# A Fourier mixing and GEGLU kernel: input tables without a setup pool, one batch's transposes in three PSUM buffers, output stores cut to multiples of sixteen rows

## The chip, the cores and the metric

One core of one Trainium2 chip. The metric is the device time of one execution in microseconds (us). The kernel before takes 1009.81 us (median of 4 runs, 1009.3 to 1010.2). Engines: PE is TensorE (PEld its weight loads), DVE VectorE, ACT ScalarE, POOL GpSimd, SP the engine that issues the output stores ("SPq" is its queue). A transfer by DMA is issued by an engine and lands when its data has arrived. An eviction copies a result of PE out of PSUM, the memory that PE writes, so that the buffer there is free again.

## The reference

```python
X = np.fft.fft(x, axis=1)          # x: (8, 3008, 256), float32
X = np.fft.fft(X, axis=2)
h = X.real.reshape(8 * 3008, 256)
g = h @ w_gate                     # (256, 1536)
gelu = 0.5 * g * (1.0 + erf(g / sqrt(2)))
out = (gelu * (h @ w_val)) @ w_out # (24064, 256), float32
```

## The kernel before

The transform over 3008 = 64 x 47 points is done with matmuls: stage 1 (64 points, table G2, result A_sb), transposes (Ap_sb), a 47-point stage (table T_PQ, result PQ_sb), and the transform over the 256 channels (tables C2 and S2, result Y_sb). A feed-forward part (ps_l, gelu_sb, h_sb, ps_o, out_sb) follows. There are eight batches. The feed-forward of batch b-1 is interleaved with the transform of batch b, so only the first transform and the last stores stand alone. These are the parts that matter (cuts marked with `# ...`):

```python
with tc.tile_pool(name="setup", bufs=1) as sp:     # released when the block ends
    # ... phases on 64 partitions, 47 x 33 columns, then the sines:
    nc.scalar.activation(G_all[:, :, 1, :], red_g, AF.Sin, scale=TWO_PI)
    # ...
    nc.scalar.activation(G_all[:, :, 0, :], red_g, AF.Sin, scale=-TWO_PI)
    nc.vector.memset(G2, 0.0)
    nc.vector.tensor_copy(...)                     # first half of G2 from G_all
    nc.sync.dma_start(                             # second half, other partitions
        out=_sub(G2, [[132, 23], [1, 66]], 66, part_start=64, part_num=64),
        in_=_sub(G_all, [[66, 23], [1, 66]], 24 * 66))
    # ... T_PQ, then C2 and S2, all with scratch of this pool

work_pool = ctx.enter_context(tc.tile_pool(name="work", bufs=1))
def x_tile():                                      # lies where the setup pool lay
    return work_pool.tile([128, 24, C], BF16, tag="x", bufs=2, name="x_sb")
def ps_tr():                                       # one buffer
    return psum_pool.tile([2 * N2, 1024], BF16, tag="tr", bufs=1, name="ps_tr")

# transposes, eight to a pack
pst = ps_tr()
for idx, (k1, cc) in enumerate(pk):
    nc.tensor.transpose(pst[:, idx * 128 : idx * 128 + 128], src, ident)
nc.scalar.activation(dst, pst[:, :n], AF.Copy)

# output of 128 tokens: cut where the row order of the output breaks
run_end = min(ue, ((ua // N2) + 1) * N2)           # N2 = 47
ln = run_end - ua                                  # mostly 47 rows or a part of 47
dst = ap_replace(out, ap=[[N1 * C, ln], [1, C]], offset=...)
nc.sync.dma_start(out=dst, in_=osb[p0 : p0 + ln, :])
```

## Time and profile before

| | before |
|---|---|
| time, median | 1009.81 us |
| first matmul | 27.19 us |
| stage 1 complete (A_sb) | 39.89 us |
| last transpose of batch 0 ends | 60.53 us |
| first matmul of the channel transform (C2) | 64.63 us |
| last matmul ends | 989.21 us |
| end of the span | 1007.72 us |

Times are from the start of the profiled span. Read the table as three pieces: 64.6 us until the channel transform begins, some 925 us that PE fills, and 18.5 us after the last matmul. The lines of the profile that carry this are shown in the prediction. One more is needed, on the output stores of the kernel before: the record of their issuing line gives the minimum, the median and the longest time, in ns, for which one issue held the queue.

```profile
L461 SPq DMA_DIRECT2D out_dram<-out_sb x696: 228/366/4578, 92.4 to 998.6; - x174
```

Half of the 696 issues are short, but the longest holds the queue for 4.6 us. Summed from the records, they hold it for 575.65 us.

### The profile page before, as it was taken

Reading aid. Unit: us, or ns where it says so; the run is one execution under the profiler, and the core shown is the slowest. Engines: PE = TensorE matmul, PEld = TensorE weight load, DVE = VectorE, ACT = ScalarE, POOL = GpSimd, SP = SyncE. Lnnn points to the kernel's source line nnn. Section 1 sums busy time; section 2 is a strip of 40 time slices with the busy share of each in tenths; the row PEclk is TensorE's granted clock in tenths of the full one; section 3 lists DMA queues with packets and bytes.
Section 4 is the critical chain, followed back from the end, with each engine's and each line's share of the span. In section 5 each row is a group of like instructions: output and inputs, shape, how many; then the busy total and the mean of one; then the engine's idle time right before and its main releaser. Section 6 shows DMA issues by size and latency. Waiting matters only on the chain.

```text
span 1007.7 us, 17222 instructions
## 1 busy us (share of the span) xinstructions
PE 943.1 (94%) x6304; PEld 611.6 (61%) x6304; DVE 590.2 (59%) x1122; ACT 502.5 (50%) x913; POOL 42.8 (4%) x81
## 2 busy tenths in 40 slices
PE   0579999999999999999999999999999999999991
PEld 0455766567656676657665676666665586555551
DVE  6457455773677547674567637765567735755550
ACT  2135554546454564555545464545545564555550
POOL 4300100010000100001000100000000000000000
PEclk9999999999999999999999999999999999999997
DMA  6900411013110411104110311101010101101110
GB/s 108 177 0 11 83 31 30 29 42 69 29 33 23 86 31 29 30 27 84 29 33 27 64 46 32 29 26 30 25 30 28 28 22 28 33 24 32 33 34 26
DMA packets 36093, 40.63 MB, mean 40 GB/s; under 512 B 5800, under 2 KB 31400, under 8 KB 36008
## 3 DMA queue, kind: packets, MB, share of 16 engines
q1 hardware_dynamic: 28792, 24.85, 8.8%
q0 software_dynamic: 7216, 14.68, 8.4%
q8 instruction: 49, 0.80, 0.3%
q14 instruction: 36, 0.29, 0.1%
HBM read 29.36 MB, written 24.64 MB: 54 GB/s over the span
## 4 chain that ended last, share of the span: by engine, by line
PE 89%; DVE 2%; DMA 2%; SPq 2%; ACT 1%; issue 1%; POOL 1%; ACTq 0%; POOLq 0%
PE ps_l L399 25%; PE ps_o L432 24%; PE ps_l L408 24%; PE ps_tr L288 8%; PE ps_dft L352 2%; PE ps_dft L344 2%; PE ps_dft L249 2%; SPq L461 2%; PE ps_dft L316 2%; DMA out_dram<-out_sb 2%; ACT Ap_sb L292 1%; DMA x_sb<-in_x_dram 1%; DVE PQ_sb L324 0%; DVE A_sb L265 0%; DVE A_sb L267 0%
## 5 line engine op out<-in xcount | busy, mean ns | idle before, releaser
L417 DVE TENSOR_TENSOR h_sb<-gelu_sb,ps_l 128x512 bf16<-128x512 bf16 (+1 forms) x576 | 386.2, 674 | 295.5 <-PE ps_l L408 144.7
L416 ACT ACTIVATE gelu_sb<-ps_l 128x512 bf16<-128x512 f32 (+1 forms) x576 | 334.1, 587 | 164.9 <-PE ps_l L399 159.9
L399 PE MATMUL ps_l<-Y_sb,Wg_sb 128*128 128x512 bf16 (+1 forms) x1152 | 342.7, 374 | 0.9
L408 PE MATMUL ps_l<-Y_sb,Wv_sb 128*128 128x512 bf16 (+1 forms) x1152 | 340.3, 374 | 0.3 <-ACT gelu_sb L416 0.3
L432 PE MATMUL ps_o<-Wo_sb,h_sb 128*128 128x256 bf16 (+1 forms) x2304 | 292.7, 272 | 2.3 <-ACT out_sb L440 1.4
L432 PEld LDWEIGHTS <-h_sb 128*128 128x128 bf16 (+1 forms) x2304 | 226.9, 99 | 68.1 <-issue 10.5
L408 PEld LDWEIGHTS <-Wv_sb 128*128 128x128 bf16 x1152 | 113.8, 100 | 114.3 <-issue 7.2
L440 ACT ACTIVATE out_sb<-ps_o 128x256 f32<-128x256 f32 x192 | 73.5, 383 | 191.1 <-PE ps_o L432 176.9
L399 PEld LDWEIGHTS <-Wg_sb 128*128 128x128 bf16 x1152 | 113.5, 102 | 79.2 <-issue 6.6
L288 PEld LDWEIGHTS <-A_sb 128*94 128x94 bf16 x528 | 99.8, 250 | 18.4 <-issue 6.9
L292 ACT ACTIVATE Ap_sb<-ps_tr 94x1024 bf16<-94x1024 bf16 (+1 forms) x72 | 68.2, 947 | 73.5 <-PE ps_tr L288 73.5
L288 PE MATMUL ps_tr<-ident,A_sb 128*94 128x128 bf16 x528 | 95.3, 311 | 7.8 <-ACT Ap_sb L292 6.8
L324 DVE CAST PQ_sb<-ps_dft 128x470 bf16<-128x470 f32 (+1 forms) x112 | 67.5, 613 | 31.9 <-PE ps_dft L316 31.9
L249 PE MATMUL ps_dft<-G,x_sb 128*128 128x132 bf16 x368 | 41.7, 232 | 32.5 <-DMA x_sb<-in_x_dram 31.4
L249 PEld LDWEIGHTS <-x_sb 128*128 128x128 bf16 x368 | 29.5, 102 | 53.1 <-issue 32.0
L362 DVE TENSOR_TENSOR Y_sb<-ps_dft,v_sb 128x470 bf16<-128x470 f32 x64 | 35.9, 560 | 42.7 <-ACT v_sb L360 42.6
L265 DVE CAST A_sb<-ps_dft 128x198 bf16<-128x198 f32 (+1 forms) x128 | 44.8, 350 | 18.5 <-PE ps_dft L249 17.7
L360 ACT ACTIVATE v_sb<-ps_dft 128x470 bf16<-128x470 f32 x64 | 31.6, 493 | 43.1 <-PE ps_dft L352 34.3
L316 PEld LDWEIGHTS <-Ap_sb 94*128 94x128 bf16 x528 | 36.5, 104 | 18.3 <-issue 0.2
L267 DVE CAST A_sb<-ps_dft 128x198 bf16<-128x198 f32 (+1 forms) x128 | 44.3, 346 | 0.0
L316 PE MATMUL ps_dft<-T_PQ,Ap_sb 94*128 94x94 bf16 x528 | 43.1, 214 | 0.1
L184 POOL DMA_DIRECT2D x_sb<-in_x_dram x32 | 17.8, 555 | 531.2 <-PE ps_dft L257 516.7
(60 smaller groups left out, 188.3 us busy)
## 6 DMA issues: line engine op xcount, KB each, us to landing
out_dram<-out_sb SPq DMA_DIRECT2D x328, 47.0 KB
x_sb<-in_x_dram POOLq DMA_DIRECT2D x56, 192.0 KB, 6.1
x_sb<-in_x_dram POOLq DMA_DIRECT2D x8, 160.0 KB, 7.7
Wg_sb<-in_moe_w_gate_dram POOLq DMA_DIRECT2D x1, 768.0 KB, 7.0
Wv_sb<-in_moe_w_val_dram POOLq DMA_DIRECT2D x1, 768.0 KB, 9.9
Wo_sb<-in_moe_w_out_dram POOLq DMA_DIRECT2D x1, 768.0 KB, 13.6
out_dram<-out_sb SPq DMA_DIRECT2D x8, 46.0 KB
out_dram<-out_sb SPq DMA_DIRECT2D x8, 45.0 KB
```

Of the source, the lines that this page charges most:

```text
L249: nc.tensor.matmul(ps[:, jj * 132 : (jj + 1) * 132], xt[:, j, cc * 128 : (cc + 1) * 128], G2[:, j, :], start=True, stop=True,)
L265: nc.vector.tensor_copy(dst, _sub(ps, [[132, np_], [1, 66]], 0))
L288: nc.tensor.transpose(pst[:, idx * 128 : idx * 128 + 128], src, ident)
L292: nc.scalar.activation(dst, pst[:, :n], AF.Copy)
L316: nc.tensor.matmul(ps[:, j * 94 : (j + 1) * 94], Ap[:, k1, cc * 128 : (cc + 1) * 128], T_PQ, start=True, stop=True,)
L324: nc.vector.tensor_copy(dst, ps[:, : g * 94])
L399: nc.tensor.matmul(psg[:, :ntok], Wg_sb[:, t, fc * 128 : (fc + 1) * 128], Yt[:, t, u0 : u0 + ntok], start=(t == 0), stop=(t == NCH - 1),)
L408: nc.tensor.matmul(psv[:, :ntok], Wv_sb[:, t, fc * 128 : (fc + 1) * 128], Yt[:, t, u0 : u0 + ntok], start=(t == 0), stop=(t == NCH - 1),)
L416: nc.scalar.activation(gl[:, :ntok], psg[:, :ntok], AF.Gelu)
L417: nc.vector.tensor_tensor(h[:, fc, :ntok], gl[:, :ntok], psv[:, :ntok], op=ALU.mult)
L432: nc.tensor.matmul(pso[:m, col0 : col0 + C], h[:, fc, sub * 128 : sub * 128 + m], Wo_sb[:, fc, :], start=(fc == 0), stop=(fc == NFC - 1),)
L440: nc.scalar.activation(osb[:m], pso[:m, col0 : col0 + C], AF.Copy)
```

## The change

The intent is to shorten both ends. At the start, the tables are made without a pool that the input's memory must wait for, and without a copy by DMA; the tables that only later stages need are made later; and the first batch's transposes get three PSUM buffers and two evicting engines. At the end, each store is cut into a multiple of 16 rows and a remainder. The diff, cut to its core:

```diff
-    G_all = const_pool.tile([N1, N2, 2, K1H], BF16)
-    G2 = const_pool.tile([128, 23, 2 * 66], BF16)
+    G2 = const_pool.tile([128, 24, 2 * 66], BF16)
-    with tc.tile_pool(name="setup", bufs=1) as sp:
-        ... (all tables, 47 x 33 columns on 64 partitions, DMA of half of G2)
+    scr_a = const_pool.tile([128, 24, K1H], FP32)     # and scr_b, scr_c, scr_d
 ...
-        for (j0, gj) in ((0, 6), (6, 6), (12, 6), (18, 6)):    # pieces of x
+        for j0 in range(0, 24, 3):
 ...
+    def ps_idle():
+        return psum_pool.tile([128, 1024], BF16, tag="l1", bufs=3, name="ps_idle")
+    ... (three iotas)
+    nc.gpsimd.memset(_sub(G2, [[132, 24], [1, 66]], 0, part_start=64, part_num=64), 0.0)
+    ... (three iotas)
+    load_x(0)
+    ... (loads of the weights, ident)
+    nc.vector.memset(_sub(G2, [[132, 24], [1, 66]], 66, part_start=0, part_num=64), 0.0)
+    ... (col_b, col_c)
+    nc.vector.tensor_scalar(row_t, row_j, col_c, 1.0 / T, op0=ALU.add, op1=ALU.mult)
+    for j in range(24):
+        nc.vector.tensor_scalar(scr_a[:, j, :], row_k, row_t[:, j : j + 1], None, op0=ALU.mult)
+    ... (reduction and four sines straight into G2)
 ...
-                pst = ps_tr()
+                pst = ps_idle() if b == 0 else ps_tr()
 ...
-                nc.scalar.activation(dst, pst[:, :n], AF.Copy)
+                if b == 0 and (pk[0][0] // 4) % 2 == 1:
+                    nc.vector.tensor_copy(dst, pst[: 2 * N2, :n])
+                else:
+                    nc.scalar.activation(dst, pst[: 2 * N2, :n], AF.Copy)
 ...
-                    nc.sync.dma_start(out=dst, in_=osb[p0 : p0 + ln, :])
+                    m16 = (ln // 16) * 16
+                    cuts = [(0, m16), (m16, ln - m16)] if hw else [(0, ln)]   # hw = True
+                    for (r0, rn) in cuts:
+                        if rn == 0:
+                            continue
+                        ... (dst of rn rows from row r0)
+                        eng.dma_start(out=dst, in_=osb[p0 + r0 : p0 + r0 + rn, :])   # nc.sync
 ...
+        if b == 0:                      # the later tables, among the work of batch 0
+            dw.insert(16, gen_tpq)
+            dw.insert(20, lambda: gen_c2s2(0))
+            dw.insert(24, lambda: gen_c2s2(1))
```

More of the change, by code (lines that the diff above doesn't have):

```diff
@@ L69 @@
     Wo_sb = const_pool.tile([128, NFC, C], BF16)
-    with tc.tile_pool(name="setup", bufs=1) as sp:
-        n1col = sp.tile([N1, 1], FP32)
-        nc.gpsimd.iota(n1col, pattern=[[0, 1]], base=0, channel_multiplier=1,
-                       allow_small_or_imprecise_dtypes=True)
-        n1scaled = sp.tile([N1, 1], FP32)
-        nc.vector.tensor_scalar(n1scaled, n1col, 1.0 / N1, None, op0=ALU.mult)
-        rowk1 = sp.tile([N1, N2, K1H], FP32)
-        nc.gpsimd.iota(rowk1, pattern=[[0, N2], [1, K1H]], base=0, channel_multiplier=0,
-                       allow_small_or_imprecise_dtypes=True)
-        rown2 = sp.tile([N1, N2, K1H], FP32)
-        nc.gpsimd.iota(rown2, pattern=[[1, N2], [0, K1H]], base=0, channel_multiplier=0,
-                       allow_small_or_imprecise_dtypes=True)
-        phase_g = sp.tile([N1, N2, K1H], FP32)
-        nc.vector.tensor_tensor(phase_g, rown2, rowk1, op=ALU.mult)
-        nc.vector.tensor_scalar(phase_g, phase_g, 1.0 / T, None, op0=ALU.mult)
-        nc.vector.scalar_tensor_tensor(phase_g, rowk1, n1scaled, phase_g,
-                                       op0=ALU.mult, op1=ALU.add)
-        tmp_g = sp.tile([N1, N2, K1H], FP32)
-        red_g = sp.tile([N1, N2, K1H], FP32)
-        nc.vector.tensor_scalar(tmp_g, phase_g, MAGIC, None, op0=ALU.add)
-        nc.vector.scalar_tensor_tensor(red_g, tmp_g, MAGIC, phase_g,
-                                       op0=ALU.subtract, op1=ALU.subtract)
-        nc.scalar.activation(G_all[:, :, 1, :], red_g, AF.Sin, scale=TWO_PI)
-        nc.vector.tensor_scalar(phase_g, phase_g, 0.25, None, op0=ALU.add)
-        nc.vector.tensor_scalar(tmp_g, phase_g, MAGIC, None, op0=ALU.add)
-        nc.vector.scalar_tensor_tensor(red_g, tmp_g, MAGIC, phase_g,
-                                       op0=ALU.subtract, op1=ALU.subtract)
-        nc.scalar.activation(G_all[:, :, 0, :], red_g, AF.Sin, scale=-TWO_PI)
-        nc.vector.memset(G2, 0.0)
-        nc.vector.tensor_copy(
-            _sub(G2, [[132, 23], [1, 66]], 0, part_start=0, part_num=64),
-            _sub(G_all, [[66, 23], [1, 66]], 0),
-        )
-        nc.sync.dma_start(
-            out=_sub(G2, [[132, 23], [1, 66]], 66, part_start=64, part_num=64),
-            in_=_sub(G_all, [[66, 23], [1, 66]], 24 * 66),
-        )
-        make_identity(nc, ident)
-        pcol94 = sp.tile([2 * N2, 1], FP32)
-        nc.gpsimd.iota(pcol94, pattern=[[0, 1]], base=0, channel_multiplier=1,
-                       allow_small_or_imprecise_dtypes=True)
-        rifl = sp.tile([2 * N2, 1], FP32)
-        nc.vector.tensor_scalar(rifl, pcol94, float(N2), None, op0=ALU.is_ge)
-        n2col = sp.tile([2 * N2, 1], FP32)
-        nc.vector.scalar_tensor_tensor(n2col, rifl, -float(N2), pcol94, op0=ALU.mult, op1=ALU.add)
-        nc.vector.tensor_scalar(n2col, n2col, 1.0 / N2, None, op0=ALU.mult)
-        ricol = sp.tile([2 * N2, 1], FP32)
-        nc.vector.tensor_scalar(ricol, rifl, -0.25, 0.25, op0=ALU.mult, op1=ALU.add)
-        rowk2 = sp.tile([2 * N2, 2, N2], FP32)
-        nc.gpsimd.iota(rowk2, pattern=[[0, 2], [1, N2]], base=0, channel_multiplier=0,
-                       allow_small_or_imprecise_dtypes=True)
-        qrow = sp.tile([2 * N2, 2, N2], FP32)
-        nc.gpsimd.iota(qrow, pattern=[[1, 2], [0, N2]], base=0, channel_multiplier=0,
-                       allow_small_or_imprecise_dtypes=True)
-        phase_t = sp.tile([2 * N2, 2, N2], FP32)
-        nc.vector.tensor_scalar(phase_t, rowk2, n2col, None, op0=ALU.mult)
-        nc.vector.scalar_tensor_tensor(phase_t, qrow, 0.25, phase_t, op0=ALU.mult, op1=ALU.add)
-        nc.vector.tensor_scalar(phase_t, phase_t, ricol, None, op0=ALU.add)
-        tmp_t = sp.tile([2 * N2, 2, N2], FP32)
-        red_t = sp.tile([2 * N2, 2, N2], FP32)
-        nc.vector.tensor_scalar(tmp_t, phase_t, MAGIC, None, op0=ALU.add)
-        nc.vector.scalar_tensor_tensor(red_t, tmp_t, MAGIC, phase_t,
-                                       op0=ALU.subtract, op1=ALU.subtract)
-        nc.scalar.activation(T_PQ[:, :], red_t, AF.Sin, scale=-TWO_PI)
-        pcol128 = sp.tile([128, 1], FP32)
-        nc.gpsimd.iota(pcol128, pattern=[[0, 1]], base=0, channel_multiplier=1,
-                       allow_small_or_imprecise_dtypes=True)
-        row256 = sp.tile([128, C], FP32)
-        nc.gpsimd.iota(row256, pattern=[[1, C]], base=0, channel_multiplier=0,
-                       allow_small_or_imprecise_dtypes=True)
-        pscal = sp.tile([128, NCH], FP32)
-        for cc in range(NCH):
-            nc.vector.tensor_scalar(pscal[:, cc : cc + 1], pcol128, float(128 * cc),
-                                    1.0 / C, op0=ALU.add, op1=ALU.mult)
-        phase_c = sp.tile([128, C], FP32)
-        tmp_c = sp.tile([128, C], FP32)
-        psin_c = sp.tile([128, C], FP32)
-        pcos_c = sp.tile([128, C], FP32)
-        xq_c = sp.tile([128, C], FP32)
-        for cc in range(NCH):
-            nc.vector.tensor_scalar(phase_c, row256, pscal[:, cc : cc + 1], None, op0=ALU.mult)
-            nc.vector.tensor_scalar(tmp_c, phase_c, MAGIC, None, op0=ALU.add)
-            nc.vector.scalar_tensor_tensor(psin_c, tmp_c, MAGIC, phase_c,
-                                           op0=ALU.subtract, op1=ALU.subtract)
-            nc.vector.tensor_scalar(xq_c, phase_c, 0.25, None, op0=ALU.add)
-            nc.vector.tensor_scalar(tmp_c, xq_c, MAGIC, None, op0=ALU.add)
-            nc.vector.scalar_tensor_tensor(pcos_c, tmp_c, MAGIC, xq_c,
-                                           op0=ALU.subtract, op1=ALU.subtract)
-            nc.scalar.activation(C2_sb[:, cc, :], pcos_c, AF.Sin, scale=-TWO_PI)
-            nc.scalar.activation(S2_sb[:, cc, :], psin_c, AF.Sin, scale=-TWO_PI)
@@ L168 @@
+    scr_a = const_pool.tile([128, 24, K1H], FP32)
+    scr_b = const_pool.tile([128, 24, K1H], FP32)
+    scr_c = const_pool.tile([128, 24, K1H], FP32)
+    scr_d = const_pool.tile([128, 24, K1H], FP32)
+    col_a = const_pool.tile([128, 1], FP32)
+    col_b = const_pool.tile([128, 1], FP32)
+    col_c = const_pool.tile([128, 1], FP32)
+    row_j = const_pool.tile([128, 24], FP32)
+    row_t = const_pool.tile([128, 24], FP32)
+    row_k = const_pool.tile([128, K1H], FP32)
     work_pool = ctx.enter_context(tc.tile_pool(name="work", bufs=1))
@@ L177, in load_x @@
         x_tiles.append(xt)
-        for (j0, gj) in ((0, 6), (6, 6), (12, 6), (18, 6)):
+        for j0 in range(0, 24, 3):
             src = ap_replace(
                 x,
-                ap=[[N2 * C, N1], [C, gj], [1, C]],
+                ap=[[N2 * C, N1], [C, 3], [1, C]],
                 offset=x.offset + (b * T + j0) * C,
             )
-            nc.gpsimd.dma_start(out=xt[0:N1, j0 : j0 + gj, :], in_=src)
-            gj2 = min(gj, 23 - j0)
+            nc.gpsimd.dma_start(out=xt[0:N1, j0 : j0 + 3, :], in_=src)
+            gj2 = min(3, 23 - j0)
             src = ap_replace(
@@ L230, in ps_tr @@
         return psum_pool.tile([2 * N2, 1024], BF16, tag="tr", bufs=1, name="ps_tr")
+    def ps_idle():
+        return psum_pool.tile([128, 1024], BF16, tag="l1", bufs=3, name="ps_idle")
+    nc.gpsimd.iota(col_a, pattern=[[0, 1]], base=0, channel_multiplier=1,
+                   allow_small_or_imprecise_dtypes=True)
+    nc.gpsimd.iota(row_j, pattern=[[1, 24]], base=0, channel_multiplier=0,
+                   allow_small_or_imprecise_dtypes=True)
+    nc.gpsimd.iota(row_k, pattern=[[1, K1H]], base=0, channel_multiplier=0,
+                   allow_small_or_imprecise_dtypes=True)
@@ new lines @@
+    rowk2_94 = const_pool.tile([2 * N2, 2, N2], FP32)
+    qrow_94 = const_pool.tile([2 * N2, 2, N2], FP32)
+    row256 = const_pool.tile([128, C], FP32)
+    nc.gpsimd.memset(_sub(G2, [[132, 24], [1, 66]], 0, part_start=64, part_num=64), 0.0)
+    nc.gpsimd.iota(rowk2_94, pattern=[[0, 2], [1, N2]], base=0, channel_multiplier=0,
+                   allow_small_or_imprecise_dtypes=True)
+    nc.gpsimd.iota(qrow_94, pattern=[[1, 2], [0, N2]], base=0, channel_multiplier=0,
+                   allow_small_or_imprecise_dtypes=True)
@@ new lines @@
+    nc.gpsimd.iota(row256, pattern=[[1, C]], base=0, channel_multiplier=0,
+                   allow_small_or_imprecise_dtypes=True)
+    load_x(0)
+    for w_hbm, w_sb in ((moe_w_gate, Wg_sb), (moe_w_val, Wv_sb)):
+        src = ap_replace(w_hbm, ap=[[F, 128], [128 * F, NCH], [1, F]], offset=w_hbm.offset)
+        nc.gpsimd.dma_start(out=w_sb, in_=src)
+    src = ap_replace(moe_w_out, ap=[[C, 128], [128 * C, NFC], [1, C]], offset=moe_w_out.offset)
+    nc.gpsimd.dma_start(out=Wo_sb, in_=src)
+    make_identity(nc, ident)
@@ new lines @@
+    nc.vector.memset(_sub(G2, [[132, 24], [1, 66]], 66, part_start=0, part_num=64), 0.0)
+    nc.vector.tensor_scalar(col_b, col_a, 64.0, -2984.0, op0=ALU.is_ge, op1=ALU.mult)
+    nc.vector.scalar_tensor_tensor(col_c, col_a, 47.0, col_b, op0=ALU.mult, op1=ALU.add)
+    nc.vector.tensor_scalar(row_t, row_j, col_c, 1.0 / T, op0=ALU.add, op1=ALU.mult)
+    for j in range(24):
+        nc.vector.tensor_scalar(scr_a[:, j, :], row_k, row_t[:, j : j + 1], None, op0=ALU.mult)
+    nc.vector.tensor_scalar(scr_b, scr_a, MAGIC, None, op0=ALU.add)
@@ new lines @@
+    nc.vector.scalar_tensor_tensor(scr_c, scr_b, MAGIC, scr_a, op0=ALU.subtract, op1=ALU.subtract)
+    for half in range(2):
+        p0 = half * 64
+        cb = half * 66
+        nc.scalar.activation(
+            _sub(G2, [[132, 24], [1, K1H]], cb + K1H, part_start=p0, part_num=64),
+            _sub(scr_c, [[K1H, 24], [1, K1H]], 0, part_start=p0, part_num=64),
+            AF.Sin, scale=TWO_PI,
+        )
+    nc.vector.tensor_scalar(scr_a, scr_a, 0.25, None, op0=ALU.add)
+    nc.vector.tensor_scalar(scr_b, scr_a, MAGIC, None, op0=ALU.add)
@@ new lines, with gen_tpq @@
+    nc.vector.scalar_tensor_tensor(scr_d, scr_b, MAGIC, scr_a, op0=ALU.subtract, op1=ALU.subtract)
+    for half in range(2):
+        p0 = half * 64
+        cb = half * 66
+        nc.scalar.activation(
+            _sub(G2, [[132, 24], [1, K1H]], cb, part_start=p0, part_num=64),
+            _sub(scr_d, [[K1H, 24], [1, K1H]], 0, part_start=p0, part_num=64),
+            AF.Sin, scale=-TWO_PI,
+        )
+    def gen_tpq():
+        pcol = col_a
+        rifl = _sub(col_b, [[1, 1]], 0, part_num=2 * N2)
+        n2col = _sub(col_c, [[1, 1]], 0, part_num=2 * N2)
+        p94 = _sub(pcol, [[1, 1]], 0, part_num=2 * N2)
+        nc.vector.tensor_scalar(rifl, p94, float(N2), None, op0=ALU.is_ge)
+        nc.vector.scalar_tensor_tensor(n2col, rifl, -float(N2), p94, op0=ALU.mult, op1=ALU.add)
+        nc.vector.tensor_scalar(n2col, n2col, 1.0 / N2, None, op0=ALU.mult)
+        ricol = _sub(col_b, [[1, 1]], 0, part_num=2 * N2)
+        nc.vector.tensor_scalar(ricol, rifl, -0.25, 0.25, op0=ALU.mult, op1=ALU.add)
+        ph = _sub(scr_a, [[1, 2 * N2]], 0, part_num=2 * N2)
+        tmp = _sub(scr_b, [[1, 2 * N2]], 0, part_num=2 * N2)
+        red = _sub(scr_c, [[1, 2 * N2]], 0, part_num=2 * N2)
+        nc.vector.tensor_scalar(ph, rowk2_94, n2col, None, op0=ALU.mult)
+        nc.vector.scalar_tensor_tensor(ph, qrow_94, 0.25, ph, op0=ALU.mult, op1=ALU.add)
+        nc.vector.tensor_scalar(ph, ph, ricol, None, op0=ALU.add)
+        nc.vector.tensor_scalar(tmp, ph, MAGIC, None, op0=ALU.add)
+        nc.vector.scalar_tensor_tensor(red, tmp, MAGIC, ph, op0=ALU.subtract, op1=ALU.subtract)
+        nc.scalar.activation(T_PQ[:, :], red, AF.Sin, scale=-TWO_PI)
@@ new lines, in gen_c2s2 @@
+    def gen_c2s2(cc):
+        pscal = col_b
+        nc.vector.tensor_scalar(pscal, col_a, float(128 * cc), 1.0 / C, op0=ALU.add, op1=ALU.mult)
+        ph = _sub(scr_a, [[1, C]], 0)
+        tmp = _sub(scr_b, [[1, C]], 0)
+        reds = _sub(scr_c, [[1, C]], 0)
+        redc = _sub(scr_d, [[1, C]], 0)
+        nc.vector.tensor_scalar(ph, row256, pscal, None, op0=ALU.mult)
+        nc.vector.tensor_scalar(tmp, ph, MAGIC, None, op0=ALU.add)
+        nc.vector.scalar_tensor_tensor(reds, tmp, MAGIC, ph, op0=ALU.subtract, op1=ALU.subtract)
+        nc.vector.tensor_scalar(ph, ph, 0.25, None, op0=ALU.add)
+        nc.vector.tensor_scalar(tmp, ph, MAGIC, None, op0=ALU.add)
+        nc.vector.scalar_tensor_tensor(redc, tmp, MAGIC, ph, op0=ALU.subtract, op1=ALU.subtract)
+        nc.scalar.activation(C2_sb[:, cc, :], redc, AF.Sin, scale=-TWO_PI)
+        nc.scalar.activation(S2_sb[:, cc, :], reds, AF.Sin, scale=-TWO_PI)
@@ L259, in run @@
                         _sub(xt, [[1, 128]], 23 * C + cc * 128, part_start=0, part_num=N1),
-                        G_all[:, 23, :, :],
+                        _sub(G2, [[1, 66]], 23 * 132, part_start=0, part_num=N1),
                         start=True,
@@ L284, in run @@
                 Ap = st["Ap"]
-                pst = ps_tr()
+                pst = ps_idle() if b == 0 else ps_tr()
                 for idx, (k1, cc) in enumerate(pk):
                     src = _sub(A, [[N2 * K1H, 2], [K1H, N2]], cc * AST + k1)
-                    nc.tensor.transpose(pst[:, idx * 128 : idx * 128 + 128], src, ident)
+                    nc.tensor.transpose(pst[: 2 * N2, idx * 128 : idx * 128 + 128], src, ident)
                 (k10, cc0) = pk[0]
@@ L455, in run @@
                         t0 = (N1 - k1) + N1 * j0
-                    dst = ap_replace(
-                        out,
-                        ap=[[N1 * C, ln], [1, C]],
-                        offset=out.offset + (b * T + t0) * C,
-                    )
-                    nc.sync.dma_start(out=dst, in_=osb[p0 : p0 + ln, :])
+                    hw = True
+                    m16 = (ln // 16) * 16
[3 more added lines that the diff above has]
+                            continue
+                        dst = ap_replace(
+                            out,
+                            ap=[[N1 * C, rn], [1, C]],
+                            offset=out.offset + (b * T + t0 + N1 * r0) * C,
+                        )
+                        eng = nc.sync if hw else nc.gpsimd
+                        eng.dma_start(out=dst, in_=osb[p0 + r0 : p0 + r0 + rn, :])
                     ua = run_end
@@ L475, in ffn_work @@
         return units
-    load_x(0)
-    for w_hbm, w_sb in ((moe_w_gate, Wg_sb), (moe_w_val, Wv_sb)):
-        src = ap_replace(w_hbm, ap=[[F, 128], [128 * F, NCH], [1, F]], offset=w_hbm.offset)
-        nc.gpsimd.dma_start(out=w_sb, in_=src)
-    src = ap_replace(moe_w_out, ap=[[C, 128], [128 * C, NFC], [1, C]], offset=moe_w_out.offset)
-    nc.gpsimd.dma_start(out=Wo_sb, in_=src)
     for b in range(B):
```

## The prediction

> **What bounds the kernel now.** I read the page's 40 slices first, to see where TensorE (PE) is not full, then a table of stretches cut at the places where the chain of work changes hands, then the waits, then the chain itself at both ends. PE is full from the third slice to the last but one, so only the two ends can give anything.
>
> ```profile
> span 1007.7 us, 17222 instructions
> PE   0579999999999999999999999999999999999991
> DVE  6457455773677547674567637765567735755550
> ```
>
> Table of stretches (length, then busy time and count of PE, weight load, DVE, ACT, POOL, then clock, DMA share, GB/s):
>
> ```profile
> 0.00:27.00 27.00, 0.00 (x0) 0.00 (x0) 17.30 (x34) 6.06 (x8) 14.07 (x26) 1.00 0.71 114
> 27.00:40.00 13.00, 7.42 (x50) 4.49 (x50) 9.04 (x34) 0.00 (x0) 4.72 (x10) 1.00 1.05 194
> 40.00:60.60 20.60, 13.85 (x97) 13.69 (x98) 3.24 (x5) 8.18 (x9) 3.32 (x7) 1.00 0.44 78
> 60.60:64.60 4.00, 3.75 (x38) 2.92 (x36) 3.87 (x8) 0.35 (x1) 0.00 (x0) 1.00 0.00 0
> 92.00:985.00 893.00, 890.87 (x5974) 576.31 (x5972) 534.99 (x994) 473.35 (x870) 20.74 (x40) 1.00 0.15 37
> 989.30:1007.80 18.50, 0.00 (x0) 0.00 (x0) 0.00 (x0) 0.38 (x1) 0.00 (x0) 0.60 0.07 25
> ```
>
> The middle, 92 to 985 us, is 890.87 of 893 us PE: nothing there can be hidden better, and the change leaves its matmuls alone. The start has 27 us with no matmul, then a stage at DVE's and the input's pace, then 20.6 us in which PE is a third idle. The end has 18.5 us with no PE work at all. The waits say why:
>
> ```profile
> POOL x_sb L184 <- ACT C_sb L165: 12.3, 1, 12.3
> PE ps_dft L249 <- DMA x_sb<-in_x_dram: 31.4, 4, 27.2
> PE ps_tr L288 <- ACT Ap_sb L292: 6.8, 8, 1.2
> ```
>
> The first line is the surprise: the first loads of x wait for the last sine (L165), though they don't use it. The x tile lies in the memory of the setup pool, so it may be written only when the last setup tile is read. Loads are issued from 22.59 us and the first matmul runs at 27.19. In the chain, transposes and their eviction alternate, because there is one buffer, ps_tr:
>
> ```profile
> 42.53 1.41 PE ps_tr L288 x8
> 43.97 1.03 ACT Ap_sb L292
> 45.04 1.42 PE ps_tr L288 x8
> 46.48 1.03 ACT Ap_sb L292
> ```
>
> So a pack takes 2.51 us of which PE works on transposes for 1.42. At the end of the chain:
>
> ```profile
> 957.91 1.89 SPq L461
> 959.84 1.94 SPq L461
> 966.12 8.74 DMA out_dram<-out_sb
> 983.47 7.26 DMA out_dram<-out_sb
> ```
>
> The output queue, not PE, is last. Issues that would take about 0.25 us hold it for 1.9, and a store lands 7 to 9 us after it is issued.
>
> [...] after 999 us its packet records show one 1 KB packet starting every 0.0425 us until 1006.0, a single engine draining; 47 such are 2.0 us, the 1.94 us that the queue stalls. [...] POOL took 0.74 to 1.04 us to issue each weight load while DVE was busy, 0.52 to 0.55 us for each load of x with DVE idle or reading PSUM; the shapes differ too. [...] the same two matmuls of 470 columns take 0.94 us at 64.6 and 0.56 us from 68.6 us.
>
> **The change, part by part.**
>
> *Tables and loads.* The tables for the first stage are made for both halves of the partitions at once (24x33 instead of 47x33 columns, no copy, no DMA of G), the others are made later, and all scratch is in the constant pool, so x waits for nothing. DVE, from 1.13 us, scaling its rows of 1551 and 256 columns (0.88 and 0.20 us between starts for a tensor_scalar, 1.68 and 0.34 for a scalar_tensor_tensor): zeroing half of G2 0.7 (1.32 us for 1518 words before, 792 now); small ones to 2.3; 24 operations of 33 columns at some 0.105 are 2.5, to 4.8; 0.5 and 0.2 of small ones, 5.5; 0.9, 6.4; then 0.5, 0.5, 0.9, to 8.3. ACT's four sines of 792 columns are 0.86 each (1.51 for 1551, 0.40 for 256): the last two end at 10.0. So the table is ready at 10 us, not at 20.5. DVE's other table work in its new order (T_PQ, a part of C2/S2, with a wait for ACT's read of scr_c) ends at 10.6.
>
> POOL: small iotas, zeroing the other half of G2 (an estimate of 1.4 us from 0.19 us for ident's 128 columns), three iotas, first x issue at 3.5 us; 16 issues at 0.52 us if undisturbed. Data moved from 1.4 us after the first issue, at 0.2 MB/us (190 to 218 KB in each full microsecond of the trace), so 1.54 MB need 7.5 us: last piece at about 14.5, or 16.5 if nine of the issues take 0.75.
>
> Stage 1 then goes at DVE's evictions: 34 of them, 4.4 us for the second 17 before (35.5 to 39.9), so 8.8, from 10.6 to 19.4. With the last x piece a little late I take 20.5, against 39.9: **19.4 us gained**.
>
> *Transposes.* ps_idle has three buffers, and DVE evicts four of nine packs (94x1024; an estimate of 1.2 us from 0.64 us for 470 and 0.36 for 198 columns). Neither ACT (1.02, and some sines of 0.4) nor DVE (1.2 and 0.9 of table work per two packs) needs the 2.84 us that PE needs for two packs. So PE sets it: 66 x 0.178 = 11.7, and in the new order of instructions only 7 of the 66 T_PQ matmuls lie between, 0.8 us: 12.5 instead of 20.6. But that order has one PQ eviction before the last transposes instead of six, so the tail of that stage grows: last transpose at 33.0, DVE free at 33.9, eight PQ evictions to the first C2 matmul, 4.2: it starts at 38.1, before at 64.63. **26.5 us gained in all at the start**, 7.1 of it here.
>
> *Stores.* Each run of rows is cut to a multiple of 16 and a remainder under 16[...]: 696 issues become 1256, but the rows on the busiest engine go from 18376 to 1704 (my count over all runs), or from 780 to 72 us at 0.0425. 1256 issues at 0.3 us are 377 us of the queue, less than the 576 us that they took before with the stalls, so no new bound. Per 128 rows there are 6 or 7 issues, 2.0 us or slightly over, for one every 1.95 us in bursts of four. At the end: PE's last matmul to the last eviction 0.4 (it waited 1.6 more for a store), backlog and four issues 1.6, landing 2.4 (0.8 from issue to first packet, 1.4 from the last packet to the end): 4.4 instead of 18.5 us. **14.1 us gained.**
>
> Sum: 26.5 + 14.1 = 40.6; 1009.8 - 40.6 = 969.2, called 969.5.
>
> **The rivals.** [...] the last piece lands at 19 and stage 1 ends at 24. For it: DVE is full just then[...]. Against it: the weights, issued while DVE was 99% busy, streamed at the full rate. It costs 3 to 4 us: 973. It also delays ident, which stands behind 19 loads on POOL. *PE warms early:* denser transposes [...] take about 0.135 us (four in 0.54 at 131.2 us): 3 us less, 966. Against it: [...]the trace shows 60 to 64 us[...] leaving it cold. *The store queue becomes the bound:* a store of 32 rows waits on one of eight semaphores; at a landing of 3 us that is 0.38 us each and a backlog of some 3 us at the end: 972. Should cutting not spread the stores, the end gains nothing: 983. *The gain at the start is given back later*, in the ramp at 77 to 92 us: weights now come after x, but the last land near 27 us and are first used near 43, so I give it little.
>
> **Range and chances.** The independent uncertainties are 3 to 4 us at the start on the slow side, 3 on the fast, and 2 to 3 at the end: 961 to 978. 2% is 20 us; either the start alone (26) gives that or the start's slow case with a small part of the end. Faster 0.97, same 0.03.
>
> **What would show it.** First matmul near 10 us, with the wait being for G2 or x and no ACT C_sb wait on POOL; A complete near 20; transposes with no wait on Ap evictions; first C2 matmul near 38; PE full after that; no store issue of 1.9 us; the end within 5 us of the last matmul. [...] I'm wrong if the first C2 matmul comes after 45, if PE's share in the middle falls under 99%, or if the last stores still take over 8 us.

## The result

| | before | after |
|---|---|---|
| time, median | 1009.76 us (13 runs, 1009.25 to 1010.2) | 972.71 us (8 runs, 972.4 to 973.55) |
| first matmul | 27.19 | 12.46 |
| stage 1 complete | 39.89 | 21.99 |
| last transpose of batch 0 ends | 60.53 | 33.12 |
| first C2 matmul | 64.63 | 39.47 |
| last matmul ends | 989.21 | 964.01 |
| end of the span | 1007.72 | 970.31 |
| from last matmul to the end | 18.5 | 6.3 |

The ratio is 0.9635, with a 95% interval of 0.9625 to 0.9644. Here and below a ratio is the mean time of one kernel's fast runs over that of the other's fast runs of the same rounds, so it is not quite the ratio of the medians quoted.

The span became 37.4 us shorter. The start gives 64.63 - 39.47 = 25.2 us of it and the end 18.5 - 6.3 = 12.2 us. The middle is unchanged: 924.6 us from the first C2 matmul to the last matmul before (989.21 - 64.63), 924.5 after (964.01 - 39.47). From the page of the kernel after, the span and PE's busy tenths in 40 slices:

```profile
span 970.3 us, 18209 instructions
PE   4999999999999999999999999999999999999996
```

The kernel before showed "057" at the left and "91" at the right. Now the first slice holds PE work, the second is full, and the last is more than half full. The table of stretches of the kernel after, cut at the same hand-overs, says what each is limited by (length, then busy time and count of PE, weight load, DVE, ACT, POOL, then clock, DMA share, GB/s):

```profile
0.00:12.40 12.40, 0.00 (x0) 0.00 (x0) 10.63 (x44) 4.98 (x6) 11.40 (x28) 1.00 0.62 90
12.40:22.00 9.60, 8.01 (x51) 4.61 (x51) 9.52 (x39) 0.53 (x2) 5.66 (x11) 1.00 1.06 186
22.00:33.10 11.10, 11.06 (x73) 11.06 (x74) 5.69 (x14) 4.99 (x7) 4.51 (x10) 1.00 1.19 182
33.10:39.50 6.40, 6.06 (x61) 4.75 (x59) 6.40 (x13) 0.38 (x1) 6.14 (x12) 1.00 1.07 166
92.00:960.00 868.00, 866.00 (x5798) 559.14 (x5797) 521.61 (x964) 460.52 (x847) 33.16 (x64) 1.00 0.16 36
964.00:970.40 6.40, 0.01 (x1) 0.00 (x0) 0.00 (x0) 0.38 (x1) 0.00 (x0) 0.76 0.15 36
```

The clock of 1.00 in the first four lines is no measurement: the trace's record of the granted clock begins only at 42.3 us, with full clock (in the kernel before at 68.2 us, so that the same holds for the early stretches in the prediction). Stage 1 (second line) is DVE's: 9.52 of 9.60 us busy. In the transposes (third line) PE is now full, 11.06 of 11.10, where it was a third idle. The fourth line is DVE's again, all 6.40 us, though PE looks busy there too. The middle is as full as before (866.00 of 868). The chain that ended last, at the start (start and length in us):

```profile
2.02 0.69 DVE row_t L175
2.82 3.60 DVE scr_a L177 x24
...
22.04 6.29 PE ps_idle L293 x37
...
32.83 0.69 DVE Ap_sb L298
33.52 5.91 DVE PQ_sb L332 x11
39.47 0.94 PE ps_dft L352 x2
...
43.25 0.57 PE ps_dft L352 x2
```

From 22.04 us the transposes no longer alternate with evictions; 37 follow each other. Two C2 matmuls still take 0.94 us at 39.47 and 0.57 only from 43.25. The end of the same chain shows the output queue:

```profile
958.63 0.32 SPq L476
...
962.58 1.46 DMA out_dram<-out_sb
```

No issue of 1.9 us is left there (the longest of the whole kernel is still 1.91 us), and a landing that the chain waits for takes 1.46 us, not 7 to 9. Two waits of the kernel after (in all, times, longest) are the ones to set against the waits of before:

```profile
ACT out_sb L448 <- DMA out_dram<-out_sb: 51.7, 46, 1.7
PE ps_dft L254 <- DVE scr_a L227: 12.5, 1, 12.5
```

POOL's wait for a sine is gone, and so is the chain's alternation with ps_tr. The second line is the wait for table G2. It names L227, an operation for a later table that merely ended at that moment; the last sine into G2 had ended at 12.21 us. The first line is new in size: the eviction of the output waits 51.7 us for its buffer to be stored, against 14.0 us in 13 waits before. It costs nothing, because ACT has room: PE waits 1.4 us in all for these evictions in both kernels, and the middle is as long as it was. Over all 1256 stores, from the record of the issuing line:

```profile
L476 SPq DMA_DIRECT2D out_dram<-out_sb x1256: 236/382/1912, 67.0 to 967.9; - x180
```

Almost twice as many issues hold the queue for 478.0 us in sum, less than the 575.65 us of before, and 22 instead of 242 take over 1 us.

### The profile page after: what moved, and what is told of

The parts are those of the page before. It is cut to its first block, busy times and chain, and to the rows that moved or that the text cites.

```text
span 970.3 us, 18209 instructions
## 1 busy us (share of the span) xinstructions
PE 943.2 (97%) x6304; PEld 610.9 (63%) x6304; DVE 588.9 (61%) x1148; ACT 498.6 (51%) x911; POOL 72.2 (7%) x144
## 4 chain that ended last, share of the span: by engine, by line
PE 94%; DVE 3%; SPq 1%; ACT 1%; DMA 1%; issue 0%; ACTq 0%; DVEq 0%
PE ps_l L407 27%; PE ps_o L440 25%; PE ps_l L416 25%; PE ps_tr L293 7%; PE ps_dft L360 2%; PE ps_dft L352 2%; PE ps_dft L254 2%; PE ps_dft L324 2%; PE ps_idle L293 1%; SPq L476 1%; DVE PQ_sb L332 1%; DMA out_dram<-out_sb 1%; DVE A_sb L272 0%; DVE A_sb L270 0%; DVE scr_a L177 0%
## 5 line engine op out<-in xcount | busy, mean ns | idle before, releaser
L293 PE MATMUL ps_tr<-ident,A_sb 128*94 128x128 bf16 x462 | 83.3, 304 | 0.0
L300 ACT ACTIVATE Ap_sb<-ps_tr 94x1024 bf16<-94x1024 bf16 (+1 forms) x63 | 59.7, 947 | 43.2 <-PE ps_tr L293 43.2
L97 POOL DMA_DIRECT2D x_sb<-in_x_dram x64 | 36.0, 562 | 473.9 <-PE ps_dft L262 468.1
L254 PE MATMUL ps_dft<-G,x_sb 128*128 128x132 bf16 x368 | 42.1, 232 | 14.2 <-DVE scr_a L227 12.5
```

The source lines that it names most:

```text
L254: nc.tensor.matmul(ps[:, jj * 132 : (jj + 1) * 132], xt[:, j, cc * 128 : (cc + 1) * 128], G2[:, j, :], start=True, stop=True,)
L293: nc.tensor.transpose(pst[: 2 * N2, idx * 128 : idx * 128 + 128], src, ident)
L300: nc.scalar.activation(dst, pst[: 2 * N2, :n], AF.Copy)
```

## The experiments

Twelve kernels ran. "After" or "before" says which kernel the edit starts from. Each time is a median of 4 runs, with 20 for the kernel that frees x alone; each ratio is to the kernel before. All results were correct.

**Is the end due to the cut of the stores, and do the two ends add?** From after, with the cut undone:

```diff
-                    m16 = (ln // 16) * 16
+                    m16 = ln
```

> The changed kernel with each run of rows stored whole again (the cut undone, nothing else). Theory (one DMA engine serves a store of 47 rows, and its backlog is the end): the gain at the end is given back and nothing else is, 972.7 + 12.2 = 985 us; queue issues of 1.9 us come back and the span ends about 18 us after the last matmul; the first C2 matmul stays at 39.5 us. Rival (the end is a fixed landing time, the gain came from elsewhere): within 2 us of 972.7.

Measured: 984.49 us (983.85 to 985.88), ratio 0.9753 [0.9737, 0.9769]. The start is unchanged (first C2 matmul at 39.46 us), and the end comes 18.1 us after the last matmul. The chain of this kernel at the end again has the lines of before:

```profile
953.55 1.93 SPq L476
...
957.79 7.38 DMA out_dram<-out_sb
```

The other direction, before with nothing but the cut:

```diff
-                    nc.sync.dma_start(out=dst, in_=osb[p0 : p0 + ln, :])
+                    m16 = (ln // 16) * 16
+                    for (r0, rn) in [(0, m16), (m16, ln - m16)]:
+                        ... (one store of rn rows from row r0)
```

> The kernel before with the stores cut alone. Theory (start and end are separate and add): 1009.8 - 12.2 = 997.6 us, the start as before (first matmul 27.2, first C2 matmul 64.6), the end 6.3 us after the last matmul. Rival (cutting also frees the middle or, the other way, its 1256 issues delay it): more than 1 us away from 997.6.

Measured: 997.95 us (997.72 to 998.33), ratio 0.9882 [0.9868, 0.9897]. The end comes 6.7 us after the last matmul and the start is that of before (C2 at 64.94 us). So the cut is worth 11.8 us with either start, and the two ends add.

**Is it the divisor, or only that stores are smaller and more?** In the traces of before and after, what follows a store depends on its row count. The landing record of each store has one update more than the largest divisor up to 16 of its row count, but never more than 16: 2 updates for 47, 41 or 23 rows, 3 for 46, 12 for 44, 16 for 15, 16, 32 or 45. So it is in all 696 stores before and all 1256 after. Whole runs also leave singly: the last 165 rows of before, parts of several stores, start one every 0.0425 us from 999.0 to 1006.0, with never more than two packets of 0.046 us open at once. In after up to 14 are open at once from 963.0 us on. A kernel with still more and still smaller stores whose divisor is low tells the divisor from size. From after, pieces of 23 rows, a prime:

```diff
-                    cuts = [(0, m16), (m16, ln - m16)] if hw else [(0, ln)]
+                    cuts = [(r0, min(23, ln - r0)) for r0 in range(0, ln, 23)]
```

> The changed kernel with each run cut into pieces of 23 rows and a remainder (47 = 23 + 23 + 1): more and shorter stores than the change makes, but 23 is prime. Theory [...]: the busiest engine gets as many rows as with whole runs or more (20992 by my count, against 18376 whole and 1704 cut), so the gain at the end is lost: 984 us or more. Rival (shorter stores, or more of them, are the gain): 972 to 974 us.

Measured: 1025.25 us (1023.22 to 1026.14), ratio 1.0153: slower than the kernel before, although the start is that of after. The stores of this kernel, as one issue's minimum, median and longest; then SP's wait for landings; then the middle stretch:

```profile
L476 SPq DMA_DIRECT2D out_dram<-out_sb x1536: 227/236/3412, 67.5 to 1016.5; - x192
```
```profile
SPq L476 <- DMA out_dram<-out_sb: 405.5, 746, 1.9
```
```profile
92.00:985.00 893.00, 860.98 (x5664) 556.25 (x5749) 517.35 (x956) 454.84 (x838) 34.17 (x66) 0.99 0.13 34
```

The median issue got shorter (236 ns), so the size isn't the matter. But SP waited 405.5 us for stores to land, and now the queue even holds up PE: 860.98 us busy of 893 where before had 890.87. Of the 52.5 us over after, 38.5 lie between the first C2 matmul and the last matmul, and 13.4 behind it. The prediction's count of rows on the busiest DMA engine divides each store's rows by that divisor and adds this up over all stores: 18376 for whole runs of rows, 20992 for pieces of 23, and 1704 for the cut of the change. It is an estimate: the records name no engine, and that all stores load the same one is taken from the 165 rows that left singly.

The number of packets on the output queue shows the divisor too. These are the lines of the pages (packets, MB, share of 16 engines) for whole runs, the change, the halves of the next experiment and the pieces of 23:

```profile
q1 hardware_dynamic: 27304, 24.65, 8.9%
q1 hardware_dynamic: 40960, 24.71, 10.2%
q1 hardware_dynamic: 33952, 24.68, 9.4%
q1 hardware_dynamic: 28048, 24.66, 7.3%
```

In each, 24064 packets are the output's rows of 1 KB. The rest, 3240, 16896, 9888 and 3984, have 4 bytes, and they are exactly the sum, over all stores, of the largest divisor up to 16 of the row count. This fits one short packet for each engine that serves a store, but the records name no engine.

That 14% more rows than with whole runs cost 40 us more is argued, not shown. At the 0.0425 us a row that the prediction read, 20992 rows are 892 us of the 949 between the first issue and the end of the last (an estimate), so that engine has hardly a pause left; 18376 rows are 781. Part of the loss is PE's clock: its record falls to half five times before the last matmul, for 27.2 us in all.

A middle case, from after, with two halves (47 = 23 + 24; 1384 stores, 10704 rows on the busiest engine by the same count):

```diff
-                    m16 = (ln // 16) * 16
+                    m16 = ln // 2
```

> The changed kernel with each run cut in two halves (47 = 23 + 24) instead of 32 + 15: about as many and as short stores. Theory [...] the stalls of the queue on pieces of 23 rows are about 1 us, and part of the backlog is left at the end: 974 to 981 us. Rival (shorter stores are the gain): equal to 972.7 within 1.

Measured: 973.98 us (973.79 to 974.12), ratio 0.9646 [0.9629, 0.9662]. That is 1.3 us over after, on the border of what the two theories expected. The end comes 7.5 us after the last matmul, against 6.3. By itself this run is inconclusive. It shows that 58% of the count of whole runs (10704 of 18376) is borne almost without loss, so the time isn't proportional to the count. Over the four ways to cut, the count (1704, 10704, 18376, 20992) and the time (972.7, 974.0, 984.5, 1025.3 us) rise together, while the number of stores (1256, 1384, 696, 1536) does not go with it.

**Are the transposes' buffers worth what the prediction said?** From after, batch 0 with one buffer and ACT alone, as in before:

```diff
-                pst = ps_idle() if b == 0 else ps_tr()
+                pst = ps_tr()
-                if b == 0 and (pk[0][0] // 4) % 2 == 1:
+                if False:
```

> The changed kernel with the first batch's transposes on the one buffer and ACT alone, as before. Theory (buffers let PE and eviction overlap): the 2.5 us period per pack comes back, from A complete to the first C2 matmul 24.7 instead of 17.5 us, so 972.7 + 7.2 = 980 us. Rival (the stage is bound by DVE's PQ evictions behind it, so that earlier transposes only wait): under 975.

Measured: 979.06 us (978.9 to 979.89), ratio 0.9696 [0.9682, 0.9711], 6.35 us over after. The chain of this kernel alternates again:

```profile
22.14 1.41 PE ps_tr L293 x7
...
23.57 1.03 ACT Ap_sb L300
```

Its first C2 matmul is at 46.73 us, 7.3 us later than in after, and 7.0 of these are left at the last matmul (970.98 against 964.01).

The change did two things here, though, and the second can be undone alone. From after, three buffers, but ACT evicts every pack:

```diff
-                if b == 0 and (pk[0][0] // 4) % 2 == 1:
+                if False:
```

> The changed kernel with its three buffers but all nine packs evicted by ACT. Theory (the buffers are the gain; ACT's 1.02 us and its few sines fit under PE's 1.36 us a pack): within 1 us of 972.7, either way. Rival (the second evicting engine is the gain): ACT sets the pace, 975 us or more.

Measured: 971.63 us (971.26 to 971.76), ratio 0.9621 [0.9606, 0.9635]. It is 1.1 us below after in the median. Each of its four runs is below each of after's eight (971.76 against 972.40), but the intervals of the two ratios overlap, so no more is claimed than that DVE's share is worth nothing. The gain is the buffers' alone. DVE is the next stage's bound, and its first C2 matmul came a little earlier without that work (39.14 against 39.47 us).

**Is it enough to free x from the setup pool?** From before, the x tiles in a pool of their own, which is opened ahead of the setup pool:

```diff
+    xin_pool = ctx.enter_context(tc.tile_pool(name="xin", bufs=1))
     with tc.tile_pool(name="setup", bufs=1) as sp:
 ...
-        return work_pool.tile([128, 24, C], BF16, tag="x", bufs=2, name="x_sb")
+        return xin_pool.tile([128, 24, C], BF16, tag="x", bufs=2, name="x_sb")
```

> The kernel before with the x tiles in memory of their own, so that x is loaded at once; tables unchanged. Theory (the shared memory costs what lies between the table and x, the slow table costs the rest): first matmul near 22.5 instead of 27.2, stage 1 at DVE's pace from there and complete at 31 instead of 39.9, so 1009.8 - 8.6 = 1001 us. Rival (the memory wait is the whole start gain of some 18 us in stage 1): 992.

Measured: 1011.1 us (1010.66 to 1011.84), ratio 1.0014 [1.0007, 1.0021]. Both the theory and its rival missed. The loads of x were issued from 7.5 us, yet the first matmul came at 31.87 us, later than in before. The chain of this kernel names what it waited for:

```profile
20.00 11.74 DMA G<-G_all
...
31.87 0.50 PE ps_dft L251 x3
```

This is the copy of half of G2 to the other partitions, 1472 packets of 132 bytes. In before its packets ran from 21.34 to 23.21 us, at a time when x was still waiting and only the last 102 packets of the weights were left. Here the first packet came 4.0 us after the issue (1.9 in before), and they ran from 23.97 to 31.35 us, taking turns with the load of Wo: from 26 to 30 us each microsecond has 250 to 253 packets of 132 bytes and as many of 512.

So I made a kernel in which that copy is undisturbed: the weights and the next batch's x are held back until G2 has landed, by copies of one column from G2 into their tiles.

```diff
+    def hold(dst):
+        nc.vector.tensor_copy(dst, G2[64:128, 22, 131:132])
 ...
+        ... (x_tile in a pool of its own, as above)
+        if b == 1: hold(xt[64:128, 0, 0:1])      # one of eight, for each piece of x
+        hold(w_sb[64:128, 0, 0:1])               # and one for Wo
         nc.gpsimd.dma_start(out=w_sb, in_=src)
```

> The kernel before with x in memory of its own, and with the weights and the second batch's x held back until the copy of G has landed (a one-column write into each of their tiles, made from G's last column, which the load then overwrites). Theory (in the run before, x was free but the copy of G, 1472 packets of 132 bytes, took 7.4 us among the weights' packets and became the wait): with the queues empty G lands near 22.5 us, the first matmul comes at about 22.7, A is complete at 31.5, and the time is 1001 to 1002 us. Rival (G's copy is slow by itself, and x's wait had hidden that): first matmul at 28 us or later, 1006 us or more.

Measured: 1003.67 us (1003.47 to 1003.88), ratio 0.9941 [0.9926, 0.9956]. The chain of this kernel:

```profile
19.56 3.73 DMA G<-G_all
...
25.09 0.37 DVE A_sb L274
```

The copy now takes 3.73 us in the chain (its packets run from 20.91 to 22.94 us, 2.0 us against 7.4), and the first matmul comes at 23.42 us. But DVE first carries out the holding copies (at most 0.15 us each in the chain, in all from 23.31 to 25.09). This kernel is some 2 us worse than the theory expected: about 1.1 us of it are these copies (an estimate: the first eviction comes 1.67 us after the first matmul, 0.59 in before), and the copy landed 0.8 us later than expected, at 23.3. With that, freeing x is worth some 6 us if the copy isn't in its way, and -1.3 us if it is. The rest of the start's gain needs the tables without that copy.

**What is left at the start?** Four kernels tried to shorten the table's chain. In the first, from after, the 24 small operations of the table become one:

```diff
-    for j in range(24):
-        nc.vector.tensor_scalar(scr_a[:, j, :], row_k, row_t[:, j : j + 1], None, op0=ALU.mult)
+    nc.vector.tensor_tensor(scr_a, _sub(row_k, [[0, 24], [1, K1H]], 0),
+                            _sub(row_t, [[1, 24], [0, K1H]], 0), op=ALU.mult)
```

> The changed kernel with the 24 multiplications of 33 columns, which took 3.6 us, made by one tensor_tensor of 792 columns. Theory (the table is still what the start waits for): it takes about 0.9 us, the first matmul comes at about 9.8 instead of 12.5, and the time falls by 2 to 2.7 us, to 970 to 970.7, provided x keeps up. Rival (x is the next limit just behind): falls by under 1 us, with stage 1 waiting for x.

Measured: 972.70 us (972.21 to 973.47), ratio 0.9633, the same as after. The first matmul came 2.6 us earlier, at 9.83 us, but a new wait took its place in the chain:

```profile
9.35 4.38 DMA x_sb<-in_x_dram
```

Stage 1 then ran at the pace of x and was complete at 21.33 us instead of 21.99. The first C2 matmul came 0.5 us earlier, and this was lost again in the middle, between 209 and 354 us; I found no cause for that.

In the second, from after, DVE and not POOL zeroes the second half of G2, so that the loads of x are issued earlier and POOL holds up nobody:

```diff
-    nc.gpsimd.memset(_sub(G2, [[132, 24], [1, 66]], 0, part_start=64, part_num=64), 0.0)
+    nc.vector.memset(_sub(G2, [[132, 24], [1, 66]], 0, part_start=64, part_num=64), 0.0)
```

> The changed kernel with the second half of G2 zeroed by DVE too instead of by POOL. Theory (DVE's row_t, 0.69 us for 24 columns, was held until POOL's zeroing ended): row_t takes about 0.15 us again and the extra 0.7 us of zeroing about cancels, first matmul within 0.4 of 12.5, 972.7 within 1; x loads start 1.4 us earlier. Rival (row_t is slow for another reason): row_t stays at 0.7 us and the start comes 0.7 us later, 973.4.

Measured: 973.84 us (973.64 to 974.41), ratio 0.9645, 1.1 us over after. Two lines of its timeline:

```profile
2.94 0.24 DVE L175 TENSOR_SCALAR row_t<-row_j,col_c 128x24 f32<-128x24 f32 x1
...
12.48 0.99 DVE L227 TENSOR_SCALAR scr_a<-row,col_b 128x256 f32<-128x256 f32 x1
```

The first is what took 0.69 us in after, beside POOL's zeroing (there from 1.26 to 2.68 us). So POOL's work had been holding up DVE. But the second takes 0.99 us where after has 0.35, at a time when POOL issues the load of Wo (12.28 to 13.35). That POOL's issue held it is argued from this coincidence and not shown: in after, a like operation took 0.29 us (12.50) while POOL issued the load of Wg. DVE also has 0.72 us more to zero. Three issues of x took 0.98 to 1.00 us here (6.58 to 8.60), where in after none took over 0.68; what held them was not tested. The first eviction came at 14.24 us, 1.0 later.

In the third, one operation instead of 24 is joined by pieces of x of six rows, so that POOL has half as many loads to issue:

```diff
-        for j0 in range(0, 24, 3):
+        for j0 in range(0, 24, 6):      # and the tensor_tensor of above
```

> The changed kernel with the one tensor_tensor for the table and x loaded in six-row pieces as before. Theory (with the table 2.6 us earlier, stage 1 was held by x in three-row pieces, which moved some 150 to 185 KB per us against 200 in six-row ones): PE's waits for x in stage 1 shrink from some 3.5 us to under 1, A is complete at 19.5 to 20.5 instead of 21.3, and the time is 970.5 to 971.8 us. Rival (the rate is HBM's or POOL's, whatever the piece): stage 1 as with three-row pieces, 972.7.

Measured: 972.45 us (972.09 to 972.86), ratio 0.9632. A_sb was complete at 21.0 us, not between 19.5 and 20.5: PE still waited 2.4 us for x in stage 1, where the theory allowed less than 1, so the longer pieces did not lift this limit. The first C2 matmul came at 38.49 us, 1 us earlier than in after. At the last matmul (964.00 us) nothing of it was left.

The fourth adds two things to the third: ACT does every second eviction of stage 1 and of PQ in batch 0, and POOL issues the remainders of the last chunk's stores.

```diff
+                # shortened; in all other cases DVE and SP as before
+                if b == 0: nc.scalar.activation(dst, src, AF.Copy)       # second half of A_sb
+                if b == 0 and (s // 5) % 2 == 1: nc.scalar.activation(dst, ps[:, : g * 94], AF.Copy)
+                eng = nc.gpsimd if (b == B - 1 and r0 > 0 and ci >= NCHUNKS - 1) else nc.sync
```

> As the run before, and in the first batch ACT makes every second eviction of stage 1 and of the PQ stage (DVE alone paced both, ACT was idle), and in the last chunk the remainders of the stores go through POOL, which is idle there. Theory: A complete at about 18.5, first C2 matmul at about 36.5 instead of 39.5, the end 5 instead of 6.3 us after the last matmul; 968 to 969 us. Rival (PE[...] is just behind DVE in both stages, and a landing of 2 us is left in any case): over 970.5.

Measured: 973.43 us (973.24 to 973.67), ratio 0.9642. This is a miss. A_sb was complete at 21.28 us and the first C2 matmul came at 38.28, where 18.5 and 36.5 were expected; PE again waited 2.4 us for x. The last matmul did end 1.05 us earlier (962.96), but the end came 9.0 us after it, not 6.3. The chain ends with POOL:

```profile
963.66 0.53 POOL out_dram L483
...
964.19 0.50 POOLq L546
```

The last packets of the stores started at 965.50 us, but the trace's record of POOL's own drain at the end of the program runs from 964.08 to 971.13 us, while SP was through at 966.4. In after the same drain follows POOL's last load in the middle of the kernel (557.48 to 561.36 us), where nobody waits for it. The work was shared well, and the engine that issued it was slow to finish. None of the twelve clearly beats after; the kernel in which ACT evicts alone comes nearest to it.

## Why the prediction was right

The prediction said 969.5 us (961 to 978) and faster with 0.97. It came to 972.71 us, by the mechanism that it named. Its gain of 40.6 us was 3 us too large; the spans show 37.4.

**The start: 26.5 us predicted, 25.2 measured.** Most single times in the sum were right. Stage 1 took 8.75 us from first to last eviction (8.8 predicted). The first load of x went out at 3.45 us (3.5). The terms that were off:

- *"24 operations of 33 columns at some 0.105 are 2.5":* they took 3.60 us in the chain, 0.15 each. With 0.69 us for row_t instead of about 0.24, DVE's part for the table ended at 10.38 us (9.39 + 0.99), not 8.3, and the table was ready at 12.2 us, not 10.0. The first rival, a late x, didn't come: the loads of x took 0.52 to 0.68 us to issue. It was DVE that was held, by POOL's zeroing (row_t 0.69 us beside it, 0.24 without).
- *"With the last x piece a little late I take 20.5":* stage 1 was complete at 21.99 us. It started 2.6 us later than predicted, and x, which was allowed 1.1 us, was not late. The run with one operation shows that it would have been, had the table come sooner: x in pieces of three rows moved 118 to 187 KB in each microsecond from 5 to 14 us, not 200. The lateness of the table hid this error.
- *The transposes, 12.5 us:* they took 11.1 (22.0 to 33.1). PE set the pace, as predicted, and 37 transposes in 6.29 us are 0.170 us each. PE didn't warm early: it was busy for 11.06 of 11.10 us from 22.0 and for 6.06 of 6.40 from 33.1, and two C2 matmuls still took 0.94 us at 39.47, against 0.57 from 43.25; the clock record begins at 42.3.
- *"eight PQ evictions to the first C2 matmul, 4.2":* it was eleven, 5.91 us. The first C2 result needs one of the three ps_dft buffers, which the code passes on in turn. With 14 PQ packs before it, that buffer is free when the twelfth is evicted, and only one had been evicted ahead of the eleven in the chain. The prediction counted only the evictions whose data is needed. The count fits the code; no run changed the number of buffers here.

That the start as a whole came so close is in part luck. The table was 2.6 us late and the last stretch, from the last transpose to the first C2 matmul, took 1.3 us more than predicted; the allowance for x (1.1) and the transposes (1.4) were too long.

The step that the prediction split as 19.4 and 7.1 us holds: with one buffer the kernel loses 6.35 us. What the prediction didn't see is that the rest isn't a sum of causes. Freeing x alone gives -1.3 us. It called the wait for the sine "the surprise", but that wait also kept the queues clear for the copy of G2. The change is right because it removes both at once.

**The end: 14.1 us predicted, 12.2 measured (11.8 in each of the two runs on the cut).** The divisor is the cause: pieces of 23 rows (1025.25 us) are slower than whole runs (984.49), and the counts of short packets agree with it exactly in four kernels. The last eviction ended 0.4 us after the last matmul, as predicted. "Backlog and four issues 1.6" is the term that was mis-sized: from the last eviction to the end of the last issue it took 3.9 us (964.42 to 968.33), and nine issues still started in it. It assumed 0.3 us an issue; the median is 0.382, and in the burst at the end one comes every 0.31 to 0.49 us. Issues took longer with a divisor of 15 than of 1: in the run with pieces of 23 rows the median is 0.229 us for stores with a divisor of 1 and 0.327 for those of 15 rows; in after it is 0.266 for one row and 0.418 for 15. So the cut that lets the rows leave side by side makes many issues longer. The third rival had the right sizes (0.38 us each, "some 3 us" of backlog) and the wrong reason: in the whole kernel SP waited only 6.4 us, in 17 waits, for landings before it issued a store (the trace has the stores on eight semaphores, 157 on each). Nor did the queue become a bound: the middle is as long as before. Landing took 2.0 us, not 2.4.

**The middle.** PE's share stayed over 99% (866.00 of 868). The gain at the start was not given back: the last matmul came 25.2 us earlier, just like the first C2 matmul.

Of the signs that were named, three came out weaker: the first matmul came at 12.46 us and not near 10, the end 6.3 us after the last matmul and not within 5, and one store issue of 1.91 us was left, with 22 over 1 us. One line was misread, without weight in the sums: PE is full from the fourth slice of the page, since the third shows 7.

Open are two things: why the 0.5 to 1 us that some experiments won at the start was lost again in the middle, and how the loss grows with the count of rows on the busiest engine between the cut of 16 and whole runs, where the halves are the only point.

## What to carry to other kernels

Before a store is issued, look at its row count: here runs of 47 rows left one row at a time, every 0.0425 us, and a cut into a multiple of sixteen and a small rest was worth 11.8 us although it made nearly twice as many stores. A wait that looks needless may shield something: when a load is set free, ask which small transfers it will now run among. And when a stage gets more buffers, look for the engine that bounds the next stage before giving it a share of the work; DVE's share of the evictions was worth nothing.
